# Half-row products in both halves of the array: a scan and gated-MLP kernel on one core

## The chip, the core and the metric

The kernel runs on one NeuronCore of a Trainium2 chip. The metric is the device time of one execution in microseconds. Engines are named as in the profile: PE is TensorE (PEld its weight loads), DVE is VectorE, ACT is ScalarE, POOL is GpSimd, SP is SyncE, which issues nearly all DMAs.

## What is computed

`x` is 2048 tokens of D = 448 features. It is normalised by token, and two branches read the result:

```python
xn = _layernorm(x, axis=-1)
s  = _A_ref(xn, ...)         # h_t = Lam_bar * h_(t-1) + B_bar @ xn_t  (448 complex states)
                             # s_t = 2 * Re(C @ h_t) + xn_t * Dskip
g  = _silu(_B_ref(xn, ...))  # (sigmoid(xn @ w_gate) * (xn @ w_up)) @ w_down, F = 1792
return x + s * g
```

All inputs and the output are bfloat16; sums are kept in fp32 in PSUM.

## The kernel before

**Chunks and tiles.** The tokens are cut into four chunks of TC = 512 (four tiles of 128). For each chunk the normalised rows xn are transposed to xnT, features on partitions: three groups of 128 and one of 64 (stored twice, on partitions 0 to 63 and 64 to 127). A *unit* is one of FT = 14 groups of 128 gate and up columns; it needs, for gate (g_ps) and for up (u_ps), three products with 128 rows (`gu_wholes`, L631) and one with 64 (`gu_halves`, L624). The two 64-row products of a unit lie in different halves of the array and run side by side. The input of the scan, bu, is cut in four parts (pt 0 to 3): parts 0 to 2 have a real and an imaginary sum, part 3 holds the last 64 states of both. They too are made of 128-row (L493) and 64-row products (L480).

**After PSUM.** ScalarE takes the sigmoid of gate (L636) and copies up (L638), VectorE multiplies them to hF (L643). ScalarE copies bu (L502), and VectorE does the scan stream of a part: it turns bu by a phase (ta, tb, sum: L508, L512, L515), runs two scans (L521), and turns back (tcs, td, h: L535, L539, L543). GpSimd computes the state carried to the next chunk (L528 to L531, three small operations). `emit_down` makes one tile of down from 14 products of hF with wd (L659, 448 columns); ScalarE takes its sigmoid and a copy (L662, L664), VectorE multiplies them to the gate g_t (L668). `emit_y` makes one tile of the output of the scan: seven products with h and ct (L681, L683) and four small products of xnT with diagonal matrices of Dskip, made by GpSimd at the start (L369), that add the skip (L687). `emit_fin` multiplies with the gate (L694), adds x (L696) and stores.

**Order.** Each chunk is a row of *sections* of two or three units (`section`, L857). The 64-row products of a section's units and of one part of bu are put together, so that a section has one stretch of 64-row products between stretches of 128-row ones. After a section follow one or two tiles of down of the chunk before; in the last sections of a chunk come output tiles of the chunk before. All of down and output of the last chunk stand at the end, in turn. `keep_order` (L930) fixes each engine's instructions in the order in which the program writes them. VectorE's scan streams are a list of pieces with planned costs; `fill` (L715) lets them out as TensorE's planned time passes. `at` and `rest` (L734, L852) put other work beside a given unit: statistics of the next chunk (`ln_plan`, L737), its normalisation on ScalarE (L246), the scaling of C into ct (`emit_c`, L434: on ScalarE c_tmp, L447; on VectorE a *mix*, L448), and the loads of x of the chunk after.

**PSUM.** Eight banks: three for gate, three for up, two ("acc") for bu, down and output in turn.

```python
for cc in range(2):
    mms(pst[cc], cc)
    act.copy(out=bus[:, cc, :], in_=pst[cc][:])
...
at(own, 1 + j, 0.8, lambda j=j: ln_stats(c * TPC + j))
at(own, 7 + j, 0.0, lambda j=j: ln_norm(c, j))
...
at(1, 6 + i // 2, 0.0, lambda i=i: mixes.append(emit_c(i)))
at(1, 7 + i // 2, 0.68, lambda: mixes.pop(0)())
```

Of the kernel before, what the change touches and what calls it, by code (L numbers as in the profile page):

```python
# [17 lines left out]
D = 448  # L18
# [45 lines left out]
def kernel(  # L64
# [32 lines left out]
    xn = [w.tile([P, TPC, DP], BF16, name=f"xn{i}") for i in range(2)]  # L97
# [14 lines left out]
    diag = w.tile([P, KT, P], BF16, name="diag")  # L112
# [14 lines left out]
    rows = w.tile([4, D], BF16, name="rows")  # L127
# [8 lines left out]
    load_row(act, 3, A_Dskip)  # L136
# [14 lines left out]
    load_x(1)  # L151

# [34 lines left out]
    warm_ps = ps.tile([P, P], FP32, name="warm_ps", tag="u", bufs=3)  # L187
# [5 lines left out]
    def turn_twice(o, src, n):  # L193

        for kt in range(3):
            pe.transpose(o[:, kt, :], src[:, kt * P:(kt + 1) * P], ident[0:n, 0:n])
        pe.transpose(o[:, 3, :], src[:, D - P:D], ident[0:n, 0:n])
        pe.transpose(o[0:64, 3, :], src[:, 384:D], ident[0:n, 0:n])
# [40 lines left out]
    def ln_norm(c, j):  # L239
        t = c * TPC + j  # L240
        xb = xn[c % 2]
# [7 lines left out]
    def ln_turn(c, j):  # L249
        xb, cols = xn[c % 2], slice(j * P, (j + 1) * P)  # L250
        if c > 0:
            sync.dma_start_transpose(out=xnT[c][:, 0:KT, cols], in_=xb[:, j, :])
            return
        for i, f0 in enumerate((0, P, 2 * P, 3 * P, D - P)):
            pe.transpose(tps[j][:, i, :], xb[:, j, f0:f0 + P], ident[:, :])  # L255

    def ln_twice(c, copy):
        copy(out=xn[c % 2][:, :, D:DP], in_=xn[c % 2][:, :, 384:D])
# [33 lines left out]
    def emit_vecs():  # L292
        tp = ps.tile([P, KT, 4], BF16, name="tp_v", tag="g", bufs=3)
        turn_twice(tp, rows, 4)
        vec = w.tile([P, KT, 4], FP32, name="vec")
        dve.tensor_copy(out=vec[:], in_=tp[:])
        dt_b = w.tile([P, KT], BF16, name="dt_b")
        act.activation(dt_b[:], vec[:, :, 0], ACT.Exp)
        K.update(dt=dt_b, lim=vec[:, :, 1], lre=vec[:, :, 2], dsk=vec[:, :, 3])
# [67 lines left out]
    def emit_diag():  # L367
        for kt in range(KT):
            pool.tensor_scalar(out=diag[:, kt, :], in0=ident[:, :], scalar1=K["dsk"][:, kt:kt + 1],  # L369
                              scalar2=None, op0=ALU.mult)  # L370
# [88 lines left out]
    def later(cost, fn, wait=0):  # L459

        pieces.append((cost, fn, wait, stream[0]))

    unread = [0]

    def bank(spare, tag, name):
        if spare:
            return ps.tile([P, TC], FP32, name=name, tag="acc", bufs=2)
        return ps.tile([P, TC], FP32, name=name, tag=tag, bufs=3)
# [5 lines left out]
    def bu_halves(c, pt):  # L474

        pst = []
        for cc in range(2 if pt < 3 else 1):
            p0, (lo, hi) = 64 * cc, bu_cols(pt, cc)
            t = bank(True, None, "bu")
# [5 lines left out]
    def emit_bu(c, pt, pst):  # L485
        unread[0] += 1
        stream[0] += 1
        popped[stream[0]] = clock[0]

        def mms(pst, cc):  # L490
            lo, hi = bu_cols(pt, cc)
            for kt in range(3):
                pe.matmul(pst[:], lhsT=bT[:, kt, lo:hi], rhs=xnT[c][:, kt, :], start=False, stop=(kt == 2))  # L493
# [4 lines left out]
        if pt < 3:  # L498
            bus = sp.tile([P, 2, TC], BF16, name="bus", bufs=4)
            for cc in range(2):  # L500
                mms(pst[cc], cc)
                act.copy(out=bus[:, cc, :], in_=pst[cc][:])  # L502
# [22 lines left out]
            def carry():  # L525
                wl = T["wv"][:, :, TC - 1:TC]
                tq = sp.tile([P, 2, 1], FP32, name="tq")
                pool.tensor_tensor(out=tq[:], in0=swap_pair(wl), in1=K["smT"][:, pt, :].unsqueeze(2), op=mul)  # L528
                tr = sp.tile([P, 2, 1], FP32, name="tr")
                pool.tensor_scalar(out=tr[:], in0=wl, scalar1=K["csT"][:, pt:pt + 1], scalar2=None, op0=mul)  # L530
                pool.tensor_tensor(out=st[pt][:], in0=tr[:], in1=tq[:], op=add)  # L531
# [23 lines left out]
            if c < NCH - 1:  # L555
                later(0.0, carry)
            for f in (p3, p4, p5):
                later(0.69, f)
        else:
            mms(pst[0], 0)  # L560
            bus = sp.tile([P, TC], BF16, name="bus3", tag="bus", bufs=4)
            act.copy(out=bus[:], in_=pst[0][:])
            bsw = sp.tile([P, TC], BF16, name="bsw3", bufs=1)
            swap_halves(bsw, bus)
# [28 lines left out]
            def q6():  # L593
                if c < NCH - 1:
                    tq = sp.tile([P, 1], FP32, name="tq3")
                    pool.tensor_tensor(out=tq[:], in0=T["ws"][:, TC - 1:TC], in1=K["sT3"][:], op=mul)
                    tr = sp.tile([P, 1], FP32, name="tr3")
                    pool.tensor_scalar(out=tr[:], in0=T["wv"][:, TC - 1:TC], scalar1=K["csT"][:, 3:4],
                                       scalar2=None, op0=mul)
                    pool.tensor_tensor(out=st3[:], in0=tr[:], in1=tq[:], op=add)  # L600
# [6 lines left out]
            for cost, f, wait in ((0.42, q0, 1), (0.42, q1, 2), (0.42, q2, 0), (1.27, q3, 0), (0.42, q4, 0),  # L607
                                  (0.42, q5, 3), (0.0, q6, 0), (0.42, q7, 0)):
                later(cost, f, wait)

# [4 lines left out]
    def emit_mul():  # L615
        if due:
            due.pop(0)()

# [15 lines left out]
    def gu_out(c, ft, gt, ub, ut=None):  # L634
# [6 lines left out]
        def mul():  # L641
            h = fp.tile([P, TC], BF16, name="hF", bufs=23)
# [3 lines left out]
        due.append(mul)  # L646

# [3 lines left out]
    def emit_gate():  # L651
        if due_g:
            due_g.pop(0)()


    def emit_down(c, j, tag="acc", bufs=2):
        d = ps.tile([P, D], FP32, name="d_ps", tag=tag, bufs=bufs)
        for ft in range(FT):
            pe.matmul(d[:], lhsT=hF[c, ft][:, j * P:(j + 1) * P], rhs=wd[:, ft, :],  # L659
                             start=(ft == 0), stop=(ft == FT - 1))  # L660
        sigd = op_.tile([P, D], BF16, name="sigd")
        act.activation(sigd[:], d[:], ACT.Sigmoid)  # L662
        zb = op_.tile([P, D], BF16, name="zb")
        act.copy(out=zb[:], in_=d[:])  # L664

        def gate():
            g = op_.tile([P, D], BF16, name="g_t", bufs=6)
            dve.tensor_tensor(out=g[:], in0=zb[:], in1=sigd[:], op=ALU.mult)  # L668
# [292 lines left out]
```

## Time and profile before

| what | value |
|---|---|
| median of three runs | 191.66 us (191.64 to 191.90) |
| the profiled execution | 191.57 us, of which the span is 189.8 us |
| chunk 1, 2, 3 on TensorE | 36.58 to 80.87, to 125.15, to 169.43 us |
| TensorE, VectorE, ScalarE busy in chunk 1 | 44.29, 40.45, 29.40 us |
| in chunk 2 | 44.28, 40.21, 25.28 us |
| in chunk 3 | 44.28, 36.39, 22.26 us |
| tail, 169.43 to 189.8: TensorE, VectorE, ScalarE busy | 16.87, 7.11, 3.87 us |
| granted TensorE clock | 1.0 |

The span is the time from the first to the last instruction of the profiled execution; its own time lies 1.77 us above it. Lines of a timeline give the start in us, the busy time in us, the engine, the line of the kernel, the operation, what it writes and reads, the size, how many were merged (x3), and in brackets for how long the engine stood idle before it and what ended the wait. A matmul's record is longer than the distance to the next start, since products follow each other in a pipeline. DMA rows on SP (SPq) show the issue, not the transfer.

### The profile page before, as it was taken

Reading aid. Unit: us, or ns where it says so; the run is one execution under the profiler, and the core shown is the slowest. Engines: PE = TensorE matmul, PEld = TensorE weight load, DVE = VectorE, ACT = ScalarE, POOL = GpSimd, SP = SyncE. Lnnn points to the kernel's source line nnn. Section 1 sums busy time; section 2 is a strip of 40 time slices with the busy share of each in tenths; the row PEclk is TensorE's granted clock in tenths of the full one; section 3 lists DMA queues with packets and bytes.
Section 4 is the critical chain, followed back from the end, with each engine's and each line's share of the span. In section 5 each row is a group of like instructions: output and inputs, shape, how many; then the busy total and the mean of one; then the engine's idle time right before and its main releaser. Section 6 shows DMA issues by size and latency. Waiting matters only on the chain.

```text
span 189.8 us, 3101 instructions
## 1 busy us (share of the span) xinstructions
PE 184.8 (97%) x1080; PEld 90.5 (48%) x1080; DVE 155.6 (82%) x315; ACT 108.5 (57%) x213; POOL 50.8 (27%) x98
## 2 busy tenths in 40 slices
PE   7999999999999999999999999999999999999992
PEld 6874433334444535444343545444444444455552
DVE  3899799958999999999998798988989792880334
ACT  4996778655679785426566766408274647223220
POOL 3785599960223320301044030200400000000000
PEclk9999999999999999999999999999999999999999
DMA  5999945994411017310010004311000000121001
GB/s 156 325 292 266 186 72 89 361 258 90 92 23 28 0 18 186 83 48 2 0 33 2 0 0 96 90 52 28 0 0 3 0 0 14 40 58 46 24 24 48
DMA packets 27591, 14.86 MB, mean 78 GB/s; under 512 B 16308, under 2 KB 27576, under 8 KB 27576
## 3 DMA queue, kind: packets, MB, share of 16 engines
q1 hardware_dynamic: 27568, 14.67, 31.6%
q8 instruction: 8, 0.13, 0.3%
q14 instruction: 7, 0.06, 0.1%
q10 hardware_dynamic: 8, 0.00, 0.0%
HBM read 8.38 MB, written 1.84 MB: 54 GB/s over the span
## 4 chain that ended last, share of the span: by engine, by line
PE 92%; DVE 4%; DMA 1%; issue 1%; POOL 0%
PE d_ps L659 22%; PE g_ps L631 19%; PE u_ps L631 19%; PE bu L493 10%; PE y_ps L681 9%; PE g_ps L624 7%; PE bu L480 2%; PE y_ps L687 2%; PE y_ps L683 1%; DMA x<-in_A_x_dram 1%; DVE xn L243 1%; DVE sg L694 1%; DVE stats L207 1%; PE tp_x L255 0%; DVE xnT L263 0%
## 5 line engine op out<-in xcount | busy, mean ns | idle before, releaser
L636 ACT ACTIVATE sig<-g_ps 128x512 bf16<-128x512 f32 x56 | 33.7, 608 | 38.8 <-PE u_ps L624 33.2
L631 PE MATMUL g_ps<-xnT,wg 128*128 128x512 bf16 (+1 forms) x180 | 46.0, 365 | 0.1
L631 PE MATMUL u_ps<-xnT,wu 128*128 128x512 bf16 (+1 forms) x180 | 45.9, 365 | 0.0
L659 PE MATMUL d_ps<-wd,hF 128*128 128x448 bf16 x224 | 44.3, 352 | 0.0
L659 PEld LDWEIGHTS <-hF 128*128 128x128 bf16 x224 | 21.7, 98 | 20.4
L638 ACT CAST ub<-u_ps 128x512 bf16<-128x512 f32 x52 | 31.0, 595 | 0.5
L631 PEld LDWEIGHTS <-wu 128*128 128x128 bf16 x180 | 17.6, 98 | 18.5
L631 PEld LDWEIGHTS <-wg 128*128 128x128 bf16 x180 | 16.8, 98 | 18.1 <-issue 1.9
L643 DVE TENSOR_TENSOR hF<-sig,ub 128x512 bf16<-128x512 bf16 x56 | 23.1, 429 | 2.5 <-ACT ub L638 2.5
L662 ACT ACTIVATE sigd<-d_ps 128x448 bf16<-128x448 f32 x16 | 8.8, 548 | 28.2 <-PE d_ps L659 28.2
L521 DVE TENSOR_TENSOR_SCAN wv<-r_col,st,ta 128x512 bf16<-128x512 f32 x18 | 22.5, 1273 | 0.3
L681 PE MATMUL y_ps<-ct,h 128*128 128x448 bf16 (+1 forms) x102 | 21.0, 342 | 0.0
L493 PE MATMUL bu<-xnT,bT 128*128 128x512 bf16 x84 | 20.9, 381 | 0.0
L528 POOL TENSOR_TENSOR tq<-wv,smT 128x2 f32<-128x2 bf16 x9 | 4.1, 460 | 47.7 <-DVE wv L521 47.7
L502 ACT CAST bus<-bu 128x512 bf16<-128x512 f32 x24 | 14.0, 588 | 4.0 <-PE bu L493 3.2
L624 PE MATMUL g_ps<-xnT,wt 64*128 64x512 bf16 (+1 forms) x60 | 15.7, 365 | 0.0
L624 PE MATMUL u_ps<-xnT,wt 64*128 64x512 bf16 (+1 forms) x60 | 15.7, 365 | 0.0
L668 DVE TENSOR_TENSOR g_t<-zb,sigd 128x448 bf16<-128x448 bf16 x16 | 6.2, 384 | 9.9 <-ACT zb L664 9.9
L493 PEld LDWEIGHTS <-bT 128*128 128x128 bf16 x84 | 6.9, 98 | 12.9 <-issue 6.8
L681 PEld LDWEIGHTS <-h 128*128 128x128 bf16 x102 | 9.4, 98 | 7.4
L207 DVE BATCH_NORM_STATS2 stats<-x 128x6 f32<-128x448 bf16 x14 | 8.6, 616 | 4.7 <-DMA x<-in_A_x_dram 4.7
L694 DVE TENSOR_TENSOR sg<-y_ps,g_t 128x448 bf16<-128x448 f32 (+1 forms) x17 | 10.0, 589 | 2.3 <-PE y_ps L687 1.9
(139 smaller groups left out, 229.2 us busy)
## 6 DMA issues: line engine op xcount, KB each, us to landing
out_dram<-o_t SPq DMA_DIRECT2D x15, 112.0 KB, 1.7
wd<-in_B_w_down_dram SPq DMA_DIRECT2D x1, 1568.0 KB, 7.9
x<-in_A_x_dram SPq DMA_DIRECT2D x3, 448.0 KB, 3.6
wg<-in_B_w_gate_dram SPq DMA_DIRECT2D x2, 384.0 KB, 4.6
wu<-in_B_w_up_dram SPq DMA_DIRECT2D x2, 384.0 KB
wg<-in_B_w_gate_dram SPq DMA_DIRECT2D x1, 576.0 KB, 4.6
wu<-in_B_w_up_dram SPq DMA_DIRECT2D x1, 576.0 KB, 6.7
bsw<-bus SPq DMA_DIRECT2D x8, 64.0 KB, 2.0
```

Of the source, the lines that this page charges most:

```text
L207: dve.bn_stats(out=stats[:], in_=x_t[t // TPC][:, t % TPC, :])
L493: pe.matmul(pst[:], lhsT=bT[:, kt, lo:hi], rhs=xnT[c][:, kt, :], start=False, stop=(kt == 2))
L502: act.copy(out=bus[:, cc, :], in_=pst[cc][:])
L521: dve.tensor_tensor_scan(out=T["wv"][:, cc, :], data0=rb, data1=T["ta"][:, cc, :], initial=(0.0 if c == 0 else st[pt][:, cc, :]), op0=mul, ...
L624: pe.matmul(t[:, n0:n1], lhsT=wt[p0:p0 + 64, f0:f1], rhs=xnT[c][p0:p0 + 64, KT if c == 0 and p0 else 3, n0:n1], start=first, stop=not first)
L631: pe.matmul(t[:, n0:n1], lhsT=wm[:, kt, f0:f1], rhs=xnT[c][:, kt, n0:n1], start=(first and kt == 0), stop=(not first and kt == 2))
L636: act.activation(sig[:], gt[:], ACT.Sigmoid)
L638: act.copy(out=ub[:], in_=ut[:])
L643: dve.tensor_tensor(out=h[:], in0=sig[:], in1=ub[:], op=ALU.mult)
L659: pe.matmul(d[:], lhsT=hF[c, ft][:, j * P:(j + 1) * P], rhs=wd[:, ft, :], start=(ft == 0), stop=(ft == FT - 1))
L681: pe.matmul(y[:, d0:d1], lhsT=hs[c, pt][:, cc, sl], rhs=ct[:, 2 * pt + cc, d0:d1], start=(pt == 0 and cc == 0), stop=False)
L694: dve.tensor_tensor(out=sg[:, d0:d1], in0=ys[c, j][:, d0:d1], in1=gs[c, j][:, d0:d1], op=ALU.mult)
```

## The change

From chunk 1 on, no product has 128 rows any more, except output in the tail. Each is cut in two with 64 rows, one in the upper half of the array (rows 0 to 63) and one in the lower. The two halves work for different sums at a time: in a *duo* of two units a and b, the upper half first does a's upper rows while the lower half does b's lower rows, and then the other way round. A sum is therefore written first by one half and then by the other. Between them the program makes GpSimd wait for the last product of the first half and pass a word to TensorE, which waits for it ahead of the other half's first product (class `Sum`; in the built program the wait stands on the weight load). Down and output of a chunk are done for all four tiles at once, with tile q in the upper half beside tile q + 2 in the lower.

- The order of chunks 1 to 3 is a list of duos (a negative number is a part of bu), with `emit_downs` third and `emit_ys` last or last but one. In the last chunk down of all four tiles comes before all of its output.
- The eight banks of PSUM are one ring. hF has 18 buffers instead of 23, the gate g_t four instead of six, xn three instead of two.
- The skip: Dskip is loaded to all partitions by one DMA on SP after x of chunk 1. VectorE multiplies xn with it in place (`emit_skip`, beside unit 9 of each chunk), and the output adds it by one product with the identity. The diagonal matrices and their load on ACT's queue go.
- The carried state is computed on VectorE, in two small operations, instead of on GpSimd.
- Statistics, normalisation and the mixes move to earlier units; the root of the variance (GpSimd's power, L232) moves beside the first tile of down.
- Chunk 0 keeps its sections. `emit_gate` is called at other places.

```diff
+    class Sum:
+        def add(self, half, lhsT, rhs, n0, n1):
+            self.done += 1
+            m = pe.matmul(self.t[:, n0:n1], lhsT=lhsT, rhs=rhs, start=self.done == 1, stop=self.done == self.n)
+            if self.half not in (None, half):
+                word = pool.nop()
+                tc.add_manual_dep(word.ins, self.ins.ins.name, SYNC, reason="the other half's last product")
+                tc.add_manual_dep(m.ins, word.ins.name, SYNC, reason="the other half's last product")
+            self.half, self.ins = half, m
+    def beside_each(top, bot):
+        for i in range(max(len(top), len(bot))):
+            for half, ops in ((0, top), (1, bot)):
+                if i < len(ops):
+                    ops[i][0].add(half, *ops[i][1])
...
+    def bu_unit(c, pt):
+        if pt < 3:
+            u.top = ops(0, 0, 4) + ops(0, 1, 3)
+            u.bot = ops(1, 0, 3) + ops(1, 1, 4)
+        else:
+            u.top, u.bot = ops(0, 0, 4), ops(1, 0, 3)
...
+    def gu_unit(c, ft):
+        u.top = ops(0, 0, 1) + ops(0, 1, 0)
+        u.bot = ops(1, 0, 0) + ops(1, 1, 1)
...
+    def emit_downs(c):
+        for q in range(TPC):
+            beside_each(ops(0, q), ops(1, (q + 2) % TPC))
+            if q >= 2:
+                empty(q - 2)
+                empty(q)
+            own = emit_mul()
+            if q == 0:
+                rest(c + 1, "down")
+            if q == 3:
+                own += emit_gate() + emit_gate()
+            fill(1.32, own)
+            fill(1.33, 0.0)
...
+    def duo(c, a, b):
+        top, bot = a.top + b.top, b.bot + a.bot
+        n = len(a.top)
+        for u, t0, t1 in ((a, 0, n), (b, n, len(top))):
+            beside_each(top[t0:t1], bot[t0:t1])
+            if u is b:
+                for i in range(2):
+                    for v in (a, b):
+                        if i < len(v.empty):
+                            v.empty[i]()
+                a.then()
+                b.then()
+            own = emit_mul() + emit_gate()
+            if u.ft is not None:
+                rest(c, u.ft)
+            fill(0.216 * (t1 - t0), own)
...
-            at(own, 1 + j, 0.8, lambda j=j: ln_stats(c * TPC + j))
-            at(own, 7 + j, 0.0, lambda j=j: ln_norm(c, j))
+            at(own, j // 2, 0.8, lambda j=j: ln_stats(c * TPC + j))
+            at(own, 4 + j, 0.0, lambda j=j: ln_norm(c, j))
...
-        at(1, 6 + i // 2, 0.0, lambda i=i: mixes.append(emit_c(i)))
-        at(1, 7 + i // 2, 0.68, lambda: mixes.pop(0)())
+        at(1, 2 + i // 2, 0.0, lambda i=i: mixes.append(emit_c(i)))
+        at(1, 3 + i // 2, 0.68, lambda: mixes.pop(0)())
...
+    for c in range(1, NCH):
+        ends = ((12, 13), emit_ys) if c == 1 else (emit_ys, (12, 13))
+        for p in ((0, -1), (1, -2), emit_downs, (2, 3), (4, -3), (5, 6), (-4, 7), (8, 9), (10, 11), *ends):
+            if callable(p):
+                p(c - 1)
+            else:
+                duo(c, *[bu_unit(c, -1 - k) if k < 0 else gu_unit(c, k) for k in p])
+    c = NCH - 1
+    emit_mul()
+    emit_mul()
+    emit_downs(c)
     flush()
+    for j in (0, 2, 1):
+        emit_y(c, j)
+        emit_gate()
+        emit_fin(c, j)
+    for d0, d1 in ((0, D // 2), (D // 2, D)):
+        emit_y(c, 3, d0, d1)
+        emit_fin(c, 3, d0, d1)
```

In a duo of two full units the sums turn from one half to the other after four or five pairs; in the duo (-4, 7), of the fourth part of bu and unit 7, the two sums of unit 7 turn after two pairs.

## The prediction

> **What bounds the kernel now.** I read the page first (busy shares, chain), then TensorE's timeline for one stretch, then VectorE's and ScalarE's timelines where the changed kernel will ask more of them.
>
> ```profile
> PE 184.8 (97%) x1080; PEld 90.5 (48%) x1080; DVE 155.6 (82%) x315; ACT 108.5 (57%) x213; POOL 50.8 (27%) x98
> ...
> PE 92%; DVE 4%; DMA 1%; issue 1%; POOL 0%
> ```
>
> TensorE is busy 97% of the span and 92% of the chain. A table of stretches gives it 44.29 us of work in the 44.29 us of chunk 1, 44.28 of 44.28 in chunks 2 and 3: no wait of TensorE is left there. What can be gained is only time inside "busy", so I look at the pitch of its products (start to start):
>
> ```profile
> 98.68 0.81 PE L631 MATMUL g_ps<-xnT,wg 128*128 128x512 bf16 x3
> 99.32 0.81 PE L631 MATMUL u_ps<-xnT,wu 128*128 128x512 bf16 x3
> 99.97 0.81 PE L631 MATMUL g_ps<-xnT,wg 128*128 128x512 bf16 x3
> 100.62 0.81 PE L631 MATMUL u_ps<-xnT,wu 128*128 128x512 bf16 x3
> 101.36 0.39 PE L624 MATMUL g_ps<-xnT,wt 64*128 64x512 bf16 x1
> 101.37 0.39 PE L624 MATMUL u_ps<-xnT,wt 64*128 64x512 bf16 x1
> 101.59 0.38 PE L624 MATMUL g_ps<-xnT,wt 64*128 64x512 bf16 x1
> ...
> 102.02 0.38 PE L480 MATMUL bu<-xnT,bT 64*128 64x512 bf16 x2
> 102.33 1.47 PE L493 MATMUL bu<-xnT,bT 128*128 128x512 bf16 x6
> ```
>
> Three whole products of 512 columns start every 0.647 us: 0.2157 each. 28 down products take 104.93 to 110.23: 0.1892 each. A pair of half products (64 rows each) starts within 0.01 us and the next pair 0.216 later, so a pair costs one whole product. But whole to half is 100.62 to 101.36, 0.74 where three products are 0.647, and half to whole is 102.02 to 102.33, 0.31 for 0.216: 0.09 lost at each turn, two turns per section, five sections per chunk.
>
> **What the change takes off TensorE.** A changed chunk has eight duos of 14 pairs and one of 11 (123 x 0.2157 = 26.53), 56 pairs of 448 columns for down (10.60) and 32 for output (6.05): 43.18 us. Before it is 44.28. Three chunks: **-3.3 us**. Two turns are left, into the first duo and into the last y: **+0.2**. Four small skip products per tile (0.20 us with L687) become one of 0.189: included. The diag products on GpSimd (L369, 4.78 us) go; they delayed nothing, so 0. The new load of skip is one more issue on SP (0.57, as L144's at 9.27) ahead of the bT transposes; the first bu product asks for those at 18.58, and SP stands idle from 24.03 to 25.36 before the next thing that matters, so it is absorbed.
>
> Each pair loads two sets of weights where a whole product loads one (1667 loads for 1080). Pairs of 256 columns start at 10.75, 10.87 and 10.98, each with two loads, so two loads fit in 0.11 us, and 448 columns leave 0.189: no loss. The Trainium skill (TensorE: Matmul & The Clock Gate, section "LDWEIGHTS (loading the stationary operand)") prices a load by its columns whatever its rows, 107 ns for 128, so that halving the rows saves nothing; two such loads in a row would not fit in 0.189, but the trace does not bear out that they stand in a row.
>
> **What it adds on TensorE: the words.** A sum may be written by one half only when the other half has finished with it. So each sum, at its turn from one half to the other, waits for a word that GpSimd sends once the other half's last product is done; the wait sits on the weight load, and everything behind it on TensorE waits too. Length of this path: product 0.376 (record), TensorE to GpSimd 0.07 (as L521's end 101.49 to L528's start 101.56), the word itself 0 to 0.1 (not in the trace), GpSimd to TensorE 0.05 (L125's end 1.29 to the first load 1.34), load 0.01 to 0.10: 0.51 to 0.70, I take 0.64. In a full duo each half's new product comes four or five pairs after the old one, 0.863 or more: hidden. In the duo with bu's fourth part the second unit's two sums turn after two pairs, 0.431: 0.08 to 0.27 each, I take 0.2, six times: **+1.2** (0.5 to 1.6). Down and output turn a whole tile later (1.5 us and more): hidden.
>
> **Chunk 1: VectorE, then ScalarE, then TensorE.** This is where I expect the loss.
>
> ```profile
> 39.73 0.68 DVE L508 TENSOR_TENSOR ta<-bus,cosT 128x1024 bf16<-128x1024 bf16 x1
> 43.28 0.63 DVE L207 BATCH_NORM_STATS2 stats<-x 128x6 f32<-128x448 bf16 x1 [2.87 <-DMA x<-in_A_x_dram]
> ```
>
> VectorE waits here for x of chunk 2, which lands at 43.25. The loads on SP are the same but for one small one (skip), so it lands then again. The change puts the four statistics of chunk 2 ahead, beside the first two units, and VectorE reaches them at about 40.1: by then it has added the skip product (1792 elements: 0.68 for 1024 and 0.42 for 512 give 1.0) and one carry (two small operations of 0.16: 0.35; bounds 0.2 to 0.5), and done less of the scan. It then stands until 43.25, with more queued behind. In the built order, between that point and the first gate of down stand, by pitches of the trace: four statistics 4 x 0.76; two hF 0.66; two carries 0.7; the rest of scan stream 1 (tcs, td, h) 1.9; root 0.1; stream 2 entire (three products 2.13, two scans 2.34, three products 1.92). Sum 12.8, so the **gate runs at 56.05**. TensorE ends the third quarter of down at 36.67 + 6.04 + 7.95 = 50.7; the sigmoid and copy buffers of down (two each) are full, and ScalarE, in order, cannot start the next tile of down before that gate.
>
> From there ScalarE's queue, with its own pitches (sig or ub 0.49, bus 0.5, c_tmp 0.565, xn 0.65):
>
> ```profile
> 55.45 0.68 ACT L447 ACTIVATE c_tmps<-tc_im,nci 128x448 f32<-128x448 bf16 x1
> 56.02 0.67 ACT L447 ACTIVATE c_tmps<-tc_re,nci 128x448 f32<-128x448 bf16 x1
> ...
> 57.70 0.75 ACT L246 ACTIVATE xn<-x,nmr,rsd 128x448 bf16<-128x448 bf16 x1
> 58.35 0.58 ACT L636 ACTIVATE sig<-g_ps 128x512 bf16<-128x512 f32 x1
> ```
>
> Gate done 56.45; two tiles of down out by 58.4; two c_tmps to 59.5; units 2 and 3 out by 61.5; four c_tmp and one xn (moved ahead here by the change) to 64.4; unit 4 with bu out from 64.4 to 66.5; then c_tmp waits for a mix on VectorE that itself waits for unit 4's product (67.1), xn, and units 5 and 6 from 68.3. TensorE, with eight banks in turn, needs them two duos later: duo (4,-3) waits for down's last bank (58.5 instead of 57.8), (bu 4th, 7) for 65.5 instead of 63.8, (8,9) for the banks of units 5 and 6 at 69.0. It ends at 72.1; without a wait it would be 68.2. **+3.9** (0 to 6: nothing if the gate came 4 us sooner; 6 if GpSimd's power operation, 1.16 us, also holds back words queued behind it and ScalarE's own overlaps fail). VectorE is still late at the end of the chunk: h3 of chunk 0 comes 0.6 after output asks for it, and the last y bank is given back 0.6 late in the next chunk: **+1.2** (0 to 1.5). Chunks 2 and 3 have no mixes and x is there; VectorE needs about 38 us of 43: no loss.
>
> **The tail.** After the last duo (start Y, end Y + 3.02) down asks at its 14th pair, Y + 5.4, for hF of unit 13. In VectorE's order it stands behind hF of 12 (its copy from PSUM done at Y + 4.0), an addition and a scan: 4.05 + 0.33 + 0.80 + 1.15 + 0.42 = Y + 6.75. **+1.35** (0 to 1.7). Before, two output tiles (166.39 to 169.43) stood between the last unit and down and covered it. The rest of the tail (four y, the last 3.6 us to the end) is as long as before.
>
> **Sum.** The profiled execution took 191.57 (span 189.8), 0.09 below the median of 191.66. 191.57 - 3.3 + 0.2 + 1.2 + 3.9 + 1.2 + 1.35 = **196.1**.
>
> **Rivals.** *ScalarE is in time* (faster): the chain from the late x does not reach TensorE. Its place is duo (4,-3) to (8,9), its price the 5.1 us of chunk 1; it decides if the first gate runs before about 52, as it would with x landing 4 us earlier. Then 196.1 - 5.1 = 191.0, and 189.8 if the words also hide everywhere. For it: VectorE's operations overlap a little in the records. Against: a 2.87 us wait that the change does not remove.
> *Words too slow*: if a word costs more than the 0.863 of four pairs, each full duo stalls twice, 24 duos; at 0.95 that is 4.2 us, about 200; none of the latencies in the trace is near it.
> *Loads in a row*: if the two loads of a pair queue up, at 98 ns each (L659's mean) they take 0.196 of 0.189, 0.007 more for 320 pairs of 448 columns: 2.2 us, 198.3. The pairs of 256 columns speak against it. By the page's 107 ns the same queue would cost 7.7 us and give 203.8.
> That the halves do not run side by side at all would show as pitches of 0.43, far above 250; the pairs at 101.36 exclude it.
>
> **How the numbers follow.** The forecast's own case 60% (193 to 199), ScalarE in time 24% (189.8 to 191.9; 17 of it faster, 7 within the bound, since tail and words stay), slow words 11%, loads 5%. A measurement of this kernel tells about 0.2% (0.4 us) from no change. Range 190.5 to 199.5: it takes in most of the second case and the loads, and leaves out the second's fast end and the slow words. Slower 0.76, same 0.07, faster 0.17.
>
> **What would show it.** TensorE's pitch 0.2157 a pair without turns: -3.3 right. In the duo with bu's fourth part two gaps of about 0.2: words right. VectorE idle about 3 us for x near 40; gate L756 first near 56; TensorE waiting for ScalarE between 57 and 70: chunk 1 right. TensorE waiting for hF some 10 us before its last down ends: tail right. I am wrong if chunk 1 takes 43 to 44 us, or if gaps stand at every duo's middle.

## The result, and the profile after

The changed kernel takes **196.28 us** (median of four runs, 196.13 to 197.18); the kernel before took 191.67 us beside it (191.64 to 191.90). A fifth run of the changed kernel on record, 195.83, is not in the median. The ratio is 1.0241, with a 95% interval of 1.0209 to 1.0273: slower by 4.6 us. The forecast was 196.1 us. That it came out on the number to 0.2 us is partly luck: errors of its terms cancelled, as shown below.

The profiled execution was the longest of the four, 197.18 us with a span of 195.4: 0.9 above the median, so the waits read from it are somewhat longer than usual. On the page the chain that ended last is no longer TensorE's alone (92% before):

```profile
PE 184.9 (95%) x1667; PEld 100.6 (51%) x1667; DVE 163.5 (84%) x343; ACT 106.5 (55%) x213; POOL 24.4 (12%) x58
...
PE 44%; DVE 29%; SPq 8%; DMA 7%; ACT 6%; issue 4%; POOL 1%; ACTq 0%; DVEq 0%
```

Chunks, from the first product of one to the first product of the next, read off TensorE's timeline:

| | chunk 1 | chunk 2 | chunk 3 | tail (last down to the end) |
|---|---|---|---|---|
| before | 44.29 | 44.28 | 44.28 | 20.37 |
| after | 48.65 | 43.74 | 43.33 | 22.61 |

So chunks 2 and 3 did get shorter, and chunk 1 and the tail gave back more than that. The table of waits (total, times, longest) names seven waits of TensorE after chunk 0; the kernel before had none:

```profile
PE d_ps L476 <- POOLq L478: 1.1, 1, 1.1
PE d_ps L476 <- DVE hF L724: 1.0, 1, 1.0
PE bu L476 <- ACT sig L727: 1.0, 1, 1.0
PE y_ps L476 <- DVE h L657: 0.6, 1, 0.6
PE g_ps L476 <- ACT sig L727: 0.6, 1, 0.6
PE u_ps L476 <- ACT zb L752: 0.5, 1, 0.5
PE u_ps L476 <- DVE sg L809: 0.4, 1, 0.4
```

The table counts from the end of the last product's record, which is 0.38 us long, while the next pair was due 0.2157 us after its start. The loss, read off the starts, is therefore larger than the number here.

**The pitch, chunk 3.** TensorE's timeline around the sixth pair of duo (-4, 7):

```profile
155.59 0.38 PE L476 MATMUL g_ps<-xnT,wg 64*128 64x512 bf16 x1
155.80 0.38 PE L476 MATMUL bu<-xnT,bT 64*128 64x512 bf16 x1
155.81 0.38 PE L476 MATMUL u_ps<-xnT,wu 64*128 64x512 bf16 x1
156.02 0.38 PE L476 MATMUL bu<-xnT,bT 64*128 64x512 bf16 x1
156.29 0.39 PE L476 MATMUL g_ps<-xnT,wg 64*128 64x512 bf16 x1
156.30 0.39 PE L476 MATMUL u_ps<-xnT,wu 64*128 64x512 bf16 x1
```

Pairs start 0.215 apart, and once 0.27: unit 7's gate changes halves there and waits 0.055 for its word. The second gap of the same size is in the same duo at 157.23. No other gap stands in chunk 3: 43.33 is, to 0.04, the 43.18 of the working plus these two gaps.

**Chunk 1.** VectorE's first statistics of chunk 2's x, and the first gate of down (the second number is the busy time, here of two gates):

```profile
44.92 0.63 DVE L208 BATCH_NORM_STATS2 stats<-x 128x6 f32<-128x448 bf16 x1 [5.54 <-DMA x<-in_A_x_dram]
...
57.52 0.69 DVE L756 TENSOR_TENSOR g_t<-zb,sigd 128x448 bf16<-128x448 bf16 x2
```

ScalarE behind it, held for 3.51 us by that gate, then late by as much with everything that follows:

```profile
53.94 0.55 ACT L752 CAST zb<-d_ps 128x448 bf16<-128x448 f32 x1
57.99 0.54 ACT L750 ACTIVATE sigd<-d_ps 128x448 bf16<-128x448 f32 x1 [3.51 <-DVE g_t L756]
...
64.97 0.80 ACT L247 ACTIVATE xn<-x,nmr,rsd 128x448 bf16<-128x448 bf16 x1
65.62 0.64 ACT L727 ACTIVATE sig<-g_ps 128x512 bf16<-128x512 f32 x1
```

The chain of waits through this stretch (start, duration, what; asked for 38 to 72 us) is one line of descent from the load to ScalarE's queue:

```profile
38.14 6.75 DMA x<-in_A_x_dram
44.92 0.64 DVE stats L208
...
52.88 2.35 DVE wv L574 x2
...
57.60 0.31 DVE g_t L756
57.95 0.04 issue
57.99 0.27 ACT sigd L750
...
59.84 1.12 ACT c_tmps L448 x2
60.95 0.97 ACT sig L727 x2
```

By starts, TensorE loses in chunk 1: 1.30 in down (words, see the first finding below), 0.98 in duo (4, -3), 1.86 in duo (-4, 7) with the two gaps of its words (0.11), 1.03 in duo (8, 9) (0.71 for a bank of gate, then 0.32 at 71.18 for one of up, which the table of waits does not list), 0.29 in output for h3; and 0.61 at the beginning of chunk 2 for the last y bank. Chunk 2 as a whole is only 0.56 longer than the 43.18, words included, so part of the 0.61 comes back.

**The tail.** VectorE's order and TensorE's wait for hF of unit 13, then for h3:

```profile
173.95 0.43 DVE L724 TENSOR_TENSOR hF<-sig,ub 128x512 bf16<-128x512 bf16 x1 [0.93 <-ACT ub L727]
174.29 0.68 DVE L568 TENSOR_TENSOR ta<-ta,tb 128x1024 bf16<-128x1024 bf16 x1
175.01 1.28 DVE L574 TENSOR_TENSOR_SCAN wv<-r_col,st,ta 128x512 bf16<-128x512 f32 x1
176.21 0.40 DVE L724 TENSOR_TENSOR hF<-sig,ub 128x512 bf16<-128x512 bf16 x1
```

```profile
176.67 8.31 PE L476 MATMUL d_ps<-wd,hF 64*128 64x448 bf16 x86 [1.04 <-DVE hF L724]
...
186.97 0.36 PE L476 MATMUL y_ps<-ct,h 128*128 128x448 bf16 x1 [0.57 <-DVE h L657]
```

Down takes 172.79 to 184.91, 12.12 for 10.60: 1.5 longer, of which the wait for hF is 1.2 by starts (175.28 to 176.67, where 0.19 was due). Then h3 costs about 0.6.

### The profile page after: what moved, and what is told of

The parts are those of the page before. It is cut to its first block, busy times and chain, and to the rows that moved or that the text cites. A ratio compares the mean times of both kernels' runs of the same rounds, so it can differ in the third digit from the quotient of the medians.

```text
span 195.4 us, 4367 instructions
## 1 busy us (share of the span) xinstructions
PE 184.9 (95%) x1667; PEld 100.6 (51%) x1667; DVE 163.5 (84%) x343; ACT 106.5 (55%) x213; POOL 24.4 (12%) x58
## 4 chain that ended last, share of the span: by engine, by line
PE 44%; DVE 29%; SPq 8%; DMA 7%; ACT 6%; issue 4%; POOL 1%; ACTq 0%; DVEq 0%
PE g_ps L476 12%; PE d_ps L476 11%; PE u_ps L476 9%; PE y_ps L476 8%; PE bu L476 5%; DVE wv L574 4%; DMA x<-in_A_x_dram 3%; SPq L253 3%; SPq L164 3%; DVE stats L208 2%; DVE hF L724 2%; DMA b_im<-in_A_B_im_dram 2%; DVE sg L809 2%; DMA wsw<-wv 2%; ACT sig L727 1%
## 5 line engine op out<-in xcount | busy, mean ns | idle before, releaser
L476 PE MATMUL u_ps<-xnT,wu 64*128 64x512 bf16 x252 | 53.6, 376 | 0.9 <-ACT zb L752 0.5
L476 PE MATMUL g_ps<-xnT,wg 64*128 64x512 bf16 x252 | 47.8, 376 | 0.7 <-ACT sig L727 0.6
L476 PE MATMUL d_ps<-wd,hF 64*128 64x448 bf16 x448 | 43.9, 349 | 2.2 <-POOLq L478 1.1
L476 PEld LDWEIGHTS <-hF 64*128 64x128 bf16 x448 | 26.2, 94 | 19.1 <-POOLq L478 1.6
L476 PE MATMUL bu<-xnT,bT 64*128 64x512 bf16 x147 | 34.8, 376 | 1.0 <-ACT sig L727 1.0
L476 PEld LDWEIGHTS <-wu 64*128 64x128 bf16 x252 | 19.8, 94 | 14.7 <-POOLq L478 1.2
L476 PEld LDWEIGHTS <-wg 64*128 64x128 bf16 x252 | 17.8, 94 | 16.2 <-issue 2.8
L476 PE MATMUL y_ps<-ct,h 64*128 64x448 bf16 (+2 forms) x203 | 24.8, 343 | 0.7 <-DVE h L657 0.6
L687 PE MATMUL g_ps<-xnT,wg 128*128 128x512 bf16 (+1 forms) x54 | 11.9, 332 | 0.2 <-DVE xnT L264 0.2
L687 PE MATMUL u_ps<-xnT,wu 128*128 128x512 bf16 (+1 forms) x54 | 11.9, 332 | 0.0
```

The lines of the kernel that those rows point to most:

```text
L476: m = pe.matmul(self.t[:, n0:n1], lhsT=lhsT, rhs=rhs, start=self.done == 1, stop=self.done == self.n)
L687: pe.matmul(t[:, n0:n1], lhsT=wm[:, kt, f0:f1], rhs=xnT[c][:, kt, n0:n1], start=(first and kt == 0), stop=(not first and kt == 2))
```

## The experiments

Duos are named as in the code's list: (4, -3) is unit 4 with bu's third part, (-4, 7) bu's fourth part with unit 7; the expectations count bu's parts from zero and call these parts 2 and 3. The main theory was the prediction's: no half product costs anything by itself; the loss comes from orders, the late x in chunk 1 and hF and the scans in the tail. Rivals: ScalarE is too full in chunk 1 whatever x does; the words or the halves cost by themselves. Every kernel is the changed kernel with the edit shown. Columns: median, ratio to the kernel before with its interval, and the chunks of the profiled execution.

| kernel | median us | ratio (95%) | chunk 1, 2, 3, tail |
|---|---|---|---|
| changed | 196.28 | 1.0241 (1.0209 to 1.0273) | 48.65, 43.74, 43.33, 22.61 |
| 1 x ahead of w_down | 193.12 | 1.0081 (1.0050 to 1.0112) | 46.40, 43.74, 43.34, 22.51 |
| 2 power late | 196.51 | 1.0233 (1.0210 to 1.0256) | 48.12, 43.74, 43.34, 22.37 |
| 3 hF of 13 early | 194.78 | 1.0156 (1.0141 to 1.0170) | 47.28, 43.74, 43.34, 21.69 |
| 4 four buffers for down | 193.49 | 1.0080 (1.0060 to 1.0100) | 45.58, 43.74, 43.35, 22.53 |
| 5 mixes back | 195.42 | 1.0201 (1.0171 to 1.0231) | 47.46, 43.41, 43.34, 22.44 |
| 6 longer words | 197.03 | 1.0273 (1.0250 to 1.0296) | 47.86, 44.09, 43.68, 23.08 |
| 7 = 1+3+4+5, scans sooner | 192.59 | 1.0051 (1.0036 to 1.0066) | 45.68, 43.41, 43.55, 21.39 |
| 8 = 7 without 1 | 193.35 | 1.0089 (1.0074 to 1.0104) | 46.38, 43.42, 43.55, 21.47 |
| 9 new order | 189.61 | 0.9908 (0.9875 to 0.9941) | 43.65, 43.12, 43.34, 20.68 |
| 10 = 7, output later | 191.67 | 1.0002 (0.9994 to 1.0011) | 45.68, 43.41, 43.35, 20.62 |
| 11 x and C ahead of w_down | 193.17 | 1.0071 (1.0050 to 1.0091) | 44.81, 43.74, 43.34, 22.46 |
| 12 = 11, output later | 192.64 | 1.0053 (1.0032 to 1.0074) | 44.56, 43.73, 43.34, 22.13 |

Part of the difference between two rows is not the edit: x does not land at the same time in every execution (last section). The landing of x is read at VectorE's first operation on it.

**1. x of chunk 2 ahead of w_down**

```diff
+    at(0, 7, 0.0, lambda: load_x(2))
...
-    at(0, 8, 0.0, lambda: (load_c(), load_x(2)))
+    at(0, 8, 0.0, load_c)
```

> The load of x for chunk 2 is issued ahead of w_down and of the C matrices instead of behind them, nothing else. Theory (VectorE stands for the late x, and everything in chunk 1 follows from that): VectorE's wait of 5.5 us goes, the first gate runs near 52 instead of 57.5, TensorE's waits between 48 and 70 go, chunk 1 takes about 43.6 instead of 48.8 us, the kernel about 191.4 us (190.8 to 192.3). Rival (ScalarE is too full in chunk 1 by the norms and the mixing operations that were moved forward, x or not): waits of 2 us or more stay between 57 and 70, and the kernel takes 194 or more. Second rival (the load only pushes w_down and C back): a new wait for w_down at the start of down, near 43.

193.12 us, between theory and rival. VectorE has no wait for x any more, the first gate runs at 53.12, and TensorE's waits for the words and in duo (4, -3) are gone. The waits of 1.03 (duo (-4, 7)) and 0.55 (8, 9) are there unchanged. In the profiled execution, the longest of this kernel (194.85 us), ScalarE stands for something else in between:

```profile
55.24 0.55 ACT L752 CAST zb<-d_ps 128x448 bf16<-128x448 f32 x1
57.53 0.67 ACT L448 ACTIVATE c_tmps<-tc_im,nci 128x448 f32<-128x448 bf16 x1 [1.74 <-issue]
```

The first mixing operation reads C transposed, whose last transposes were issued from 51.09 instead of 49.84, behind loads that are now later. No wait for w_down arose.

**2. The power operation after the last quarter of down**

```diff
-            if q == 0:
+            if q == 3:
                 rest(c + 1, "down")
```

> The power operation of chunk 2 and 3 (and the small addition ahead of it) is issued after the last quarter of down instead of after the first. It waits for VectorE, and the words of down's second half stand behind it on GpSimd: TensorE waited 1.1 us for them at 48.5. Theory (the gate on VectorE is what sets the pace, the words only wait for the same late VectorE): the wait of 1.1 us goes, and the wait for down's last bank in duo (4, bu part 2) grows by as much; the kernel stays within 0.4 us of 196.3. Rival (the words behind the power are a loss of their own): 195.2.

196.51 us: no change, as expected, but not by the wait that was named. The words' wait left down and came back in the next duo, longer, because VectorE's small addition now stood behind the second scan. GpSimd and TensorE:

```profile
57.03 1.11 POOL L233 TENSOR_TENSOR rsd<-ve,mhalf 128x4 f32<-128x4 f32 x1 [20.78 <-DVE ve L232]
```

```profile
57.06 0.91 PE L476 MATMUL g_ps<-xnT,wg 64*128 64x512 bf16 x6 [1.81 <-POOLq L478]
```

Wherever the power waits for VectorE, the words queued behind it wait too.

**3. hF of unit 13 ahead of the scan, in the last duo**

```diff
             own = emit_mul() + emit_gate()
+            if c == NCH - 1 and u.ft == 13:
+                own += emit_mul()
```

> In the last duo VectorE does the product hF of unit 13 right behind that of unit 12, ahead of an addition and a scan. By the step of the prediction (down waits for hF, the rest of the tail is as before) the kernel gains 1.35 us: 194.9. Theory now, from the trace after (VectorE's scan work of chunk 3 runs on into the tail to 186.9 and output waits for h3 at its eighth product): down ends 1.3 to 1.5 us earlier, the wait for h3 grows from 0.6 to about 2 us, and the kernel gains 0 to 0.3 us.

194.78 us, 0.8% under the changed kernel. The tail is 21.69 instead of 22.61: 0.92 gained. Down is 10.89 long (12.12 before the edit), and of the 1.23 that this gives, h3 takes back 0.29: its wait grows from 0.57 to 0.86. So the step on record (1.35 for hF) holds nearly, and the theory formed from the trace after, which left almost no gain, fails. It read h3 as fixed by VectorE's scans, but in the profiled execution of the changed kernel h3 also waited for the swap of wv by DMA, 3.1 us from issue to landing, against 2.0 in the other chunks and in this kernel. So part of the gain is that shorter swap, which the edit did not aim at (last section): in this kernel, too, VectorE's product td for h3 waits for the swap (1.35 us), so by estimate a swap of 3.1 would have put h3 about 1.1 us later. What is left of the 0.8% may be x, which landed at 43.25 in the profiled execution, so that the words cost nothing there.

**4. Four buffers for the sigmoid and the copy of down**

```diff
-            sigd = op_.tile([P, D], BF16, name="sigd")
+            sigd = op_.tile([P, D], BF16, name="sigd", bufs=4)
...
-            zb = op_.tile([P, D], BF16, name="zb")
+            zb = op_.tile([P, D], BF16, name="zb", bufs=4)
```

> Four buffers instead of two for the sigmoid and the copy of down, so that ScalarE empties all four tiles of down without waiting for a gate. x still comes late. Theory (the gate holds ScalarE, and ScalarE the banks): ScalarE's wait of 3.5 us at 54.5 goes, so do TensorE's waits for ScalarE between 58 and 70 (3.0 us in sum), the 1.1 us for the words stay; 193.5 us (193.0 to 194.3). Rival (VectorE's lateness sets the end of chunk 1 by h3 whatever ScalarE does): waits move to the output's h3, 195.8 or more.

193.49 us against 193.5: the hold works as thought. x is as late as ever (44.27, gate at 56.88), yet ScalarE goes from down straight on to the mixing operations:

```profile
55.95 0.55 ACT L752 CAST zb<-d_ps 128x448 bf16<-128x448 f32 x1
56.36 0.70 ACT L448 ACTIVATE c_tmps<-tc_im,nci 128x448 f32<-128x448 bf16 x1
```

Of TensorE's waits in chunk 1, those for zb and for sig in duo (-4, 7) are gone; the words' (0.76) and that in (8, 9) (0.47) stay.

**5. The mixing operations back to where they were**

```diff
-        at(1, 2 + i // 2, 0.0, lambda i=i: mixes.append(emit_c(i)))
-        at(1, 3 + i // 2, 0.68, lambda: mixes.pop(0)())
+        at(1, 6 + i // 2, 0.0, lambda i=i: mixes.append(emit_c(i)))
+        at(1, 7 + i // 2, 0.68, lambda: mixes.pop(0)())
```

> The seven mixing operations of C (ScalarE's c_tmp, VectorE's ct) are issued from units 6 and 7 of chunk 1 on, where the kernel before had them, instead of from units 2 and 3. x still comes late, down still has two buffers. Theory (two causes side by side: the late x costs the words' wait and the wait in duo (4, bu part 2); the mixing operations in ScalarE's queue cost the waits in duos (bu part 3, 7) and (8, 9)): these last two, 1.4 and 0.7 us beyond TensorE's pitch, go, the first two stay: 194.3 us (193.8 to 195.3). Rival (ScalarE's work has to be done somewhere in chunk 1, the waits only move to duo (10, 11) or to output): 195.8 or more.

195.42 us: mostly the rival. The waits in duo (-4, 7) and (8, 9) go, and as many come at output, for sig and for h3 (0.48 and 0.61 in the table of waits; by starts output and its first banks lose some 2.5 us). The chunk is 47.46 long, 1.2 shorter than in the changed kernel, but the words' wait alone is 1.0 shorter in this execution (x landed at 43.73). The medians' intervals overlap. Moving this work within the busy duos gains nothing that can be told here.

**6. Longer words**

```diff
+    dot = w.tile([P, 1], FP32, name="dot")
...
-                word = pool.nop()
+                word = pool.memset(dot[:], 0.0)
```

> Each word is sent by a small GpSimd operation (one element per partition set to zero) instead of a bare semaphore instruction, which makes the path of a word longer by the time of that operation; nothing else. Small operations of GpSimd take 0.2 to 0.6 us in the trace, so the path goes from 0.49 to some 0.7 to 1.1 us. Theory (a word costs only what its path is longer than the pairs between the two halves of a sum, 0.43 us in the duo with bu part 3 and 0.86 in the full ones): the gaps of 0.06 us in the duos with bu part 3 grow by the operation's time, and full duos show none as long as the path stays under 0.86: 196.9 us (196.5 to 197.8) if the operation takes 0.2 to 0.35, and two gaps in every full duo of chunks 2 and 3 beyond that. Rival (words cost nothing at all, the gaps of 0.06 us are something else): 196.3, gaps unchanged.

The operation takes 0.099 us (the trace's row of it), less than the 0.2 to 0.6 that was expected. In the trace the two gaps of duo (-4, 7) go from 0.055 to 0.22 each (starts 111.52 and 111.96, 112.62 and 113.06), in chunk 3 as well (43.68 for 43.33); no full duo shows a gap. The median is 0.75 us over the changed kernel's, with intervals that overlap. The path of a bare word is therefore 0.431 + 0.055 = 0.49 us from the start of the old half's last product to the start of the new half's first, and 0.65 with the operation, 0.165 more for an operation recorded with 0.099; both are well under the 0.863 of a full duo. The rival (gaps that are not the words') is out.

**7 and 8. All repairs at once, and the same with x where it was**

7 has the edits of 1, 3, 4 and 5, and gives VectorE's scan pieces of chunk 3 out sooner; 8 leaves out that of 1.

```diff
-            fill(0.216 * (t1 - t0), own)
+            fill(0.216 * (t1 - t0) + (0.3 if c == NCH - 1 else 0.0), own)
```

> Together: x of chunk 2 loaded ahead of w_down and C; four buffers for the sigmoid and the copy of down; the mixing operations from unit 6 on; in the last duo hF of unit 13 right behind that of 12; in chunk 3 the pieces of the scan given out 0.3 us sooner per half duo. Theory (the loss is these orders and not the halves): chunk 1 and 2 43.5 to 43.9 us each, no wait of TensorE in chunk 1, tail 21 us, 189.9 us (189.2 to 190.8), faster than the kernel before. Rival (the halves themselves cost: words, weight loads): 191.5 or more with waits spread over all chunks.

> As the kernel with all repairs, but x of chunk 2 is loaded where the changed kernel loads it, behind C. What is left of the late x when ScalarE has buffers and a short queue: theory, only the words behind the power operation, 0 to 1.1 us by how late x lands: 190.6 us (189.9 to 191.4). Rival (the late x is the main cause by itself): 192 or more.

192.59 and 193.35 us: both theories were 2.7 us too low. Against each other they say what was asked: with room on ScalarE the late x costs 0.76 us. But 7 still has 45.68 in chunk 1 and 21.39 in the tail, and its waits are those that experiment 5 had made, and hF:

```profile
PE y_ps L476 <- DVE h L657: 0.6, 1, 0.6
PE y_ps L476 <- ACT sig L727: 0.5, 1, 0.5
PE d_ps L476 <- DVE hF L724: 0.5, 1, 0.5
```

The mixing operations need a stretch where ScalarE is idle. There is one: 6.75 us during down (44.22 to 50.97 in this kernel), if C is there by then.

**9. A new order**

```diff
+    at(0, 7, 0.0, lambda: (load_x(2), load_c()))
...
-    at(0, 8, 0.0, lambda: (load_c(), load_x(2)))
...
-    for i in range(7):
-        at(1, 2 + i // 2, 0.0, lambda i=i: mixes.append(emit_c(i)))
-        at(1, 3 + i // 2, 0.68, lambda: mixes.pop(0)())
+    for i, t0, t1 in ((1, "down", 3), (3, "down", 3), (5, "down", 4), (0, 3, 5), (2, 3, 6), (4, 6, 7), (6, 8, 9)):
+        at(1, t0, 0.0, lambda i=i: mixes.append(emit_c(i)))
+        at(1, t1, 0.68, lambda: mixes.pop(0)())
...
-        ends = ((12, 13), emit_ys) if c == 1 else (emit_ys, (12, 13))
+        ends = ((12, 13), emit_ys) if c in (1, NCH - 1) else (emit_ys, (12, 13))
```

with the edits of 3, 4 and 7, and both buffers of c_tmps made with the first mixing operation.

> All repairs in a new order: x of chunk 2 and C are loaded ahead of w_down; three of the seven mixing operations run on ScalarE while TensorE does down, the others spread over units 3 to 8, VectorE's parts over units 3 to 9; four buffers for down; chunk 3's scan pieces sooner; hF of 13 right behind 12; and in chunk 3 output of chunk 2 stands behind the last duo instead of ahead of it, so that it lies between the last units and down. Theory (what the kernel with all repairs still loses is 1.9 us in chunk 1, where ScalarE's mixing operations hold sig and h3, and 1.0 us in the tail, where down waits for hF): both go, 189.7 us (189.0 to 190.8), about 1 percent faster than the kernel before. Rival (w_down comes too late behind x and C): a wait for w_down of 1 us or more in the first tile of down near 43. Rival (halves cost something else): 191.5 or more.

**189.61 us against 189.7, 0.9% faster than the kernel before** (ratio 0.9908, 0.9875 to 0.9941; its six runs go from 188.99 to 191.08). The page shows TensorE busy 97% again, and the table of waits nothing after chunk 0:

```profile
PE 182.4 (97%) x1664; PEld 99.9 (53%) x1667; DVE 163.3 (87%) x343; ACT 106.4 (57%) x213; POOL 24.4 (13%) x58
```

The chunks are 43.65, 43.12 and 43.34, within 0.5 us of the 43.18 of the working. Three mixing operations now run before down is emptied:

```profile
51.70 0.67 ACT L449 ACTIVATE c_tmps<-tc_re,nci 128x448 f32<-128x448 bf16 x1 [5.30 <-DMA tc_im<-c_im]
52.27 0.65 ACT L449 ACTIVATE c_tmp<-tc_re,nci 128x448 f32<-128x448 bf16 x1
52.83 0.52 ACT L751 ACTIVATE sigd<-d_ps 128x448 bf16<-128x448 f32 x1
```

**10. Kernel 7 with output of chunk 2 behind the last duo** (the last line of the edit of 9)

> As the first kernel with all repairs (192.6 us), and in chunk 3 output of chunk 2 behind the last duo. Theory (the tail loses because nothing lies between the last units and down): 1.0 us less, 191.6 us (191.2 to 191.9). Rival (VectorE's scans and output products pile up in the tail whatever the order): 192.4 or more, with waits for h of chunk 3 or for banks.

191.67 us: the tail is 20.62 for 21.39, and the 0.9 us is as expected. The edit covers hF, and the kernel stands level with the one before (1.0002).

**11 and 12. Only the loads; the loads and the order of output**

> One edit to the changed kernel: x of chunk 2 and C are both loaded ahead of w_down (x alone ahead of w_down gave 193.1 us, and ScalarE then stood 1.74 us for C, which had been pushed back). Order of all engines as in the changed kernel. By the second case of the prediction (the chain from the late x does not reach TensorE once the first gate runs 4 us sooner) all 5.1 us of chunk 1 go: 191.2 us or less, no wait of TensorE for ScalarE left in chunk 1. Theory now: the gate runs near 53, ScalarE starts the mixing operations near 55.8 instead of 57.5, the wait in the duo with bu part 3 shrinks from 1.86 to 0.1 to 0.3 us, that in duo (8, 9) of 0.7 stays, because a c_tmp there waits for a mix on VectorE: 191.4 us (190.9 to 192.2), chunk 1 44.2 to 44.8 us. Rival (ScalarE has too much in these duos whatever the loads do): chunk 1 46 us, 193 or more.

> Two edits to the changed kernel: the loads as in the kernel before this one, and in chunk 3 output of chunk 2 behind the last duo instead of ahead of it. Theory: the tail, 22.5 us with output ahead, comes to 20.7 as in the two kernels that had this order: 1.8 us less than with the loads alone, 189.6 us (189.0 to 190.6), as fast as the kernel with all repairs. Rival (the tail needs the sooner scan pieces and the early hF of unit 13 as well): tail 21.5 or more, 190.6 or more.

193.17 us for 11. Its chunk 1 is what the theory gave, 44.81, with the wait in duo (-4, 7) gone and of ScalarE's only that in (8, 9) left (0.46 in the table, 0.93 by starts, behind a mix on VectorE). Its time missed the theory's 191.4. The kernel is no faster than 1: the 1.74 us of ScalarE's wait for C, which this edit removes, had been read in an execution of kernel 1 that was 1.7 us over its own median. So 11 shows that the wait went with C's place in the queue. That C was not late in most executions of kernel 1 would explain the equal medians, but is not shown: one execution of each has a profile. 192.64 us for 12, within the rival's case: the tail is 22.13, because hF of unit 13 now stood behind the four output products of chunk 2 in VectorE's order, and down waited for it:

```profile
172.06 0.41 DVE L724 TENSOR_TENSOR hF<-sig,ub 128x512 bf16<-128x512 bf16 x1
```

```profile
172.53 1.31 PE L476 MATMUL d_ps<-wd,hF 64*128 64x448 bf16 x12 [1.33 <-DVE hF L724]
```

Six us of other products between the units and down help only if VectorE's order lets hF through.

## Why the prediction was right, step by step

| step | predicted | in the profiled execution |
|---|---|---|
| turns between whole and half products | -3.3 + 0.2 | -3.1, confirmed |
| words, six gaps | +1.2 | +0.33 |
| words behind the power | 0 (a bound of the range) | +1.30 |
| banks of ScalarE, chunk 1, without the gaps of words | +3.9 | +3.76 |
| h3 and the last y bank | +1.2 | +0.90 |
| tail, without its turn | +1.35 | +2.15 |
| chunk 0 | 0 | +0.39 |

The sum is 5.7 for the 5.6 us between the two spans; part of the 0.61 for the last y bank comes back. The terms that were too large (words, banks, h3 and y) had 1.3 us too much, the others 2.5 too little, and the median of the changed kernel is 0.9 below this execution. That these three nearly cancel is luck. Start times of chunk 1 in the experiments' profiles lie between 36.69 and 37.10, so the 0.39 of chunk 0 is mostly scatter.

**Turns: right.** Pairs of 512 columns keep 0.2157, down's pairs 0.189 (56 in 10.60), and kernel 9 shows three chunks within 0.5 us of that pace. The rival of loads in a row is out. The pitch alone would not decide it, since two loads of 94 ns just fit in 0.189. But the page shows that the loads of a pair overlap: down's 448 loads of 94 ns are 42.1 us one after another, and cover 26.2 (the number behind the bar).

```profile
L476 PEld LDWEIGHTS <-hF 64*128 64x128 bf16 x448 | 26.2, 94 | 19.1 <-POOLq L478 1.6
```

The Trainium skill's page "TensorE: Matmul & The Clock Gate", section "LDWEIGHTS (loading the stationary operand)", prices a load by its columns alone, whatever its rows; an estimate by its formula is 107 ns for 128 columns, where the rows have 94. The Trainium skill's page "TensorEngine Tiling (Array Packing)", section "Key Properties", says that different tiles of the array can load and multiply in parallel, and that a change of tiling mode drains the array. The rows agree with the first: the loads overlap, with no loss per pair. Each turn costs 0.09 us here; that this is the drain no row shows.

**Words: the step failed in size.** The estimate of the path, "0.51 to 0.70, I take 0.64", was too long. It is 0.49 by the gaps of the changed kernel. Experiment 6 shows that the gaps are the words', but not the 0.49 a second time: there the path grew by 0.165, and the operation is recorded with 0.099. The gap of two pairs (0.431) hid all but 0.055.

**Words behind the power: a hidden wait.** The forecast thought of GpSimd's 1.16 us and set it in the range. What counted is less that time than that the power waits for VectorE, which waits for x; the words of down's third tile stood behind it. So the price goes with the landing of x. In kernels with this order, x landing and wait (table of waits): 43.25, none; 43.73, 0.17; 44.14, 0.44; 44.27, 0.76; 44.92, 1.13.

**Chunk 1: right, as a chain and nearly as a size.** The forecast had 12.8 us from x to the first gate. Measured in the seven kernels with this order of loads: 12.59 (x at 43.25) to 12.61 (44.27), and 12.60 in the changed kernel (44.92). Duo (4, -3) lost 0.98 (0.7 expected), duo (-4, 7) 1.86 (1.7), (8, 9) 1.03 (1.5). In kernel 3, where x came at 43.25 as forecast, the three lose as much: its chunk 1 of 47.28 is 43.18 plus 0.28 for h3, 0.11 for words and 3.7 for these banks. Experiment 4, which frees ScalarE and leaves x late, and experiment 1, which does the opposite, give back 2.8 and 3.2 us: gate and buffers are two links of one chain. The claim in the range, "nothing if the gate came 4 us sooner", failed: with the gate 4.4 us sooner the wait in (8, 9) stays, and what ScalarE has to mix in these duos only moves (experiment 5) until it goes where ScalarE is idle (9).

**x "lands then again" at 43.25: not quite.** It did in one of seven profiled executions with this order of loads (kernel 3), and came 0.5 to 1.7 later in the others.

**Tail: right for hF, incomplete.** hF cost 1.2 (1.35 expected): by so much is down shorter in experiment 3. The sentence "the rest of the tail is as long as before" is the part that failed: VectorE's scans of chunk 3 ran 14 us into the tail, to 186.91 (before, the last h was done at 168.58, ahead of it), and output waited about 0.6 for h3.

**The rivals.** ScalarE in time did not happen, since x did not come sooner. Given that x, experiment 11 shows where it would have ended: chunk 1 at 44.81 and 193.2 us, not 191.0, because (8, 9) keeps its wait and the tail loses 2.1 instead of 1.35. Its gate ran at 52.96, a little behind the 52 that the rival named. Slow words are excluded by a path of 0.49 against 0.863.

## What to carry to other kernels

Packing TensorE's products closer moves its neighbours' deadlines; before counting the gain, list for every engine in order what stands ahead of the operation that gives a PSUM bank back, and which load that first one waits for. A load that was late without harm becomes the bound as soon as someone in an in-order queue asks for it earlier, and a message sent by a queue that has another wait in it is as late as that wait. Work without a deadline (here the mixing of C) is best put where its engine is idle and its data already there, and in a tail VectorE's order counts as much as TensorE's.

## What the runs showed of the hardware

- A bare word is released when the operation ahead of it on GpSimd starts, not when it ends: the power started at 49.67 and ran 1.41 us, TensorE went on at 49.71. Kernels 2, 4, 5 and 8 show the same, 0.03 to 0.04 us behind the start of the power. A word that is an operation waits for the end: in kernel 6 TensorE went on at 50.01, after the power (48.49 to 49.90). Both views, of the changed kernel and then of kernel 6:

```profile
49.67 1.41 POOL L233 TENSOR_TENSOR rsd<-ve,mhalf 128x4 f32<-128x4 f32 x1 [13.48 <-DVE ve L232]
```

```profile
48.49 1.41 POOL L233 TENSOR_TENSOR rsd<-ve,mhalf 128x4 f32<-128x4 f32 x1 [6.63 <-DVE ve L232]
49.86 0.56 POOL L479 MEMSET dot<- 128x1 f32 x4
```

- The bare word itself is recorded with 17 ns; a message between the halves by way of GpSimd, from one product's start to the next one's, takes 0.49 us.
- The same load, issued behind the same others, lands up to 1.7 us apart between executions (43.25 to 44.92 in seven kernels). The cause stays open.
- The last swap of wv by DMA took 2.0 us in six kernels (3, 7, 8, 9, 10, 12) and 2.8 to 3.2 in the other seven, the changed kernel among them. In all seven a transfer on another queue, which the profile lists as "instruction" (q8, one packet of 16 KB), ran beside it, in none of the six. No run moved that transfer on purpose. The queues, the issue and its time to landing, of the changed kernel and then of kernel 3:

```profile
q1 hardware_dynamic: 160, 0.13, 16.7%
q8 instruction: 1, 0.02, 3.1%
wsw<-wv SPq DMA_DIRECT2D x2, 64.0 KB, 3.1
```

```profile
q1 hardware_dynamic: 160, 0.13, 19.0%
wsw<-wv SPq DMA_DIRECT2D x1, 64.0 KB, 2.0
```

- Why some kernels spread more than others stays open: only one execution of each has a profile. The late x alone is not the reason: the four runs of kernel 8, with x late, spread over 0.1%, and those of kernels 1, 9 and 11, with x early, over 1.0 to 1.2% (192.09 to 194.06 for the twelve of 11). Kernels 7, 8 and 10, with four buffers for down and the mixing operations late, stay within 0.1 to 0.2%; the moment at which C arrives for the mixing operations is a candidate that no run tests.
